# A fused attention and two feed-forward layers on one core: loads issued by two queues, mask patterns on two engines, and another block order at the start

## The chip, the cores and the metric

The kernel runs on one core of a Trainium2 chip, as one launch. The metric is device time in microseconds (us); the figure given for a kernel is the median of its runs. The engines are TensorE (PE in the profile; its weight loads are PEld), VectorE (DVE), ScalarE (ACT), GpSimd (POOL) and SyncE (SP), which here does little but issue DMA transfers.

## What is computed

All inputs are float32, but for two int64 words and the weights, which are float64.

```python
def _attn_ref(q, k, v, n_global, n_local):          # q, k, v: (2, 8, 768, 64)
    scores = scale * np.matmul(q, k.transpose(0, 1, 3, 2))
    rel = pos[:, None] - pos[None, :]
    is_global = pos[None, :] < int(n_global)         # 8
    is_local = (rel >= 0) & (rel < int(n_local))     # 96
    keep = is_global | is_local
    dist = np.where(is_global & ~is_local, float(n_local), np.abs(rel))
    slopes = 2.0 ** (-8.0 * (np.arange(H) + 1) / H)
    scores = np.where(keep, scores - slopes[:, None, None] * dist[None, :, :], -1000000000.0)
    ... softmax over the keys, times v ...
def _moe_ref(x, w_in, w_out):                        # (1536, 512) x (512, 2048), then x (2048, 512)
    h = x @ w_in
    return (h * (1.0 / (1.0 + np.exp(-h)))) @ w_out
def _moe2_ref(x, w_in, w_out):
    h = x @ w_in
    return (h * np.clip(h + 3.0, 0.0, 6.0) / 6.0) @ w_out
```

The result is `_moe2_ref(_moe_ref(attention))`.

## The kernel before

**Attention.** A query sees only the keys of the last 96 positions and the first 8, so the work goes in units: one batch entry, one half of the sequence (384 positions, three blocks of 128) and one pair of heads. There are 16 units, four pairs of heads for each half. A block of queries is scored against 256 columns (the 96 positions ahead of the block, 32 global keys, and its own 128 keys), or, for block 0 of a first half, against 128 (`width`). One loop counts slots `n`; slot `n` belongs to unit `n // 3`, step `n % 3`.

- `loads(u)` issues a unit's keys (`rk`, two transfers, one for each head), earlier keys (`kp`) and queries (`rq`, two transfers). Units 0, 1 and 2 are loaded ahead of the loop, unit u + 3 in unit u's step 1. `loads_v` does the values.
- `stage_a(u, 0)` transposes the keys on TensorE and copies them on ScalarE (L350, tile `kt`), `stage_a(u, 1)` the queries (L331, tile `qt`). Unit u + 1 is staged during unit u. `scores(u)`, at step 0, waits for `kt` and `qt`. It writes blocks 0 and 1 of a head into one PSUM bank (tag S) and block 2 into another (tag o). A matmul in float32 takes two passes, each an instruction of its own in the profile, so a unit's scores are 12 instructions.
- `exponentials(u, t)` adds the bias of block `t` on VectorE and takes the row minimum (L379, tile `z`, the negated scores), then ScalarE takes the exponential (L383). `normalise` divides on GpSimd (L393), blocks 0 and 1 at step 1, block 2 at step 2. `turn` transposes a unit's weights one unit later and `values` multiplies them by v.

**Mask patterns.** `positions` and `patterns` make two masks of distances from the words `n_global` and `n_local`, which the program reads at run time: `distA` (256 columns) and `distB` (128 columns, for block 0 of a first half). In `patterns` every step is VectorE's (L277 to L295). The temporaries lie in the two buffers of tile `z`, which units 0 and 1 take over. `biases(p)` multiplies both masks by the slopes of a head pair on GpSimd (L314, tiles `nbA` and `nbB`). `beyond` (L300 to L305) sets a flag for a general fallback; it is called in slot 30, and what reads the flag comes in slot 77.

**Weights.** The weights are float64 words and are decoded by hand in pieces of 128 x 512: ScalarE takes the absolute value (`upper`, L103) and the low word (`lower`, L107), VectorE shifts and masks (L992 to L1009), GpSimd multiplies and adds (L126, L134). Each step of a piece is put into a slot; `ahead` (L734) says how many slots before the piece's first use its decoding begins. For the first piece `ahead` is PRE = 17, so it begins in slot 0. Raw pieces have two buffers, and three pieces are requested ahead of the loop.

**Feed-forward.** From slot 17 on, pieces of the first layer's matmuls (`h_piece`, `y_piece`) are put between the attention steps; after the attention they fill the program to its end. Each product is done as three, with high and low parts of the operands.

**Order.** Within the attention loop the instructions of TensorE, ScalarE and GpSimd keep the order of the program; those of VectorE and SyncE are placed by a planner ahead of the launch. After it VectorE too keeps the program's order. Instructions of the loop can be placed between those that are written ahead of it. Each engine executes its list in order.

Of the kernel before, what the change touches and what calls it, by code (L numbers as in the profile page):

```python
# [12 lines left out]
I32 = mybir.dt.int32  # L13
# [15 lines left out]
def attention_ffn_kernel(ctx, tc, q, k, v, n_global, n_local, w_in1, w_out1, w_in2, w_out2, out):  # L29
# [17 lines left out]
    ident = keep.tile([P, P], F32, name="ident", tag="ident")  # L47
    nval = keep.tile([P, 2], F32, name="nval", tag="nval")
    flag = keep.tile([P, 1], I32, name="flag", tag="flag")
    three = keep.tile([P, 1], F32, name="three", tag="three")  # L50

    main = ExitStack()
# [102 lines left out]
    def fast(l, c):  # L155

        return c > (2, 1)[l]
# [61 lines left out]
    W = 2 * P  # L219
    SP = P + G  # L220

    def loads(u):
        b, half, p = units[u]
        s0 = half * TB
        rk = apool.tile([P, HB, 2, D], F32, name=f"rk{u}", tag="rk")
        kp = apool.tile([P, 2, D], F32, name=f"kp{u}", tag="kp")
        rq = apool.tile([P, HB, 2, D], F32, name=f"rq{u}", tag="rq")
        hs = slice(2 * p, 2 * p + 2)
        for h in range(2):
            nc.sync.dma_start(rk[:, :, h, :], k[b, 2 * p + h, s0:s0 + TB].rearrange("(t p) d -> p t d", p=P))  # L230
        if half:
            nc.sync.dma_start(kp[:G0], k[b, hs, s0 - G0:s0, :].rearrange("h p d -> p h d"))
            nc.sync.dma_start(kp[G0:], k[b, hs, :G, :].rearrange("h p d -> p h d"))
        else:
            nc.sync.dma_start(kp[:G], k[b, hs, :G, :].rearrange("h p d -> p h d"))
        for h in range(2):
            nc.sync.dma_start(rq[:, :, h, :], q[b, 2 * p + h, s0:s0 + TB].rearrange("(t p) d -> p t d", p=P))
        raw[u] = [rk, kp, rq, None, None]

    def loads_v(u):  # L240
# [15 lines left out]
    slopes = [2.0 ** (-8.0 * (h + 1) / H) for h in range(H)]  # L256
    FAR = 1e9 / slopes[-1]

    small = cpool.tile([P, 5], F32, name="small", tag="small")
    t1 = apool.tile([P, HB, 2, W], F32, name="pat1", tag="z", bufs=ZB)[:, 0]  # L260
    t2 = apool.tile([P, HB, 2, W], F32, name="pat2", tag="z", bufs=ZB)[:, 0]
    rel, tmp, glob, col = distA, t2[:, 0, :], t2[:, 1, :P], t2[:, 1, P:]

    def positions():

        reli, coli = t1[:, 0, :].bitcast(I32), t1[:, 1, :P].bitcast(I32)
        nc.gpsimd.iota(reli[:, :P], pattern=[[-1, P]], base=G0, channel_multiplier=1)
        nc.gpsimd.iota(reli[:, P:], pattern=[[-1, P]], base=0, channel_multiplier=1)
        nc.gpsimd.iota(coli, pattern=[[1, P]], base=0, channel_multiplier=0)
        nc.vector.tensor_copy(rel, reli)  # L270
        nc.vector.tensor_copy(col, coli)
        nc.vector.tensor_scalar(out=tmp, in0=rel, scalar1=0.0, scalar2=None, op0=ALU.is_ge)

    def patterns():

        low, up, high = nwords[:, :, 0], nwords[:, :, 1], small[:, 0:2]
        nc.vector.scalar_tensor_tensor(out=high, in0=low, scalar=0.0, in1=up, op0=ALU.is_lt, op1=ALU.add)  # L277
        nc.vector.scalar_tensor_tensor(out=nval, in0=high, scalar=4294967296.0, in1=low, op0=ALU.mult, op1=ALU.add)
        ng, nl = nval[:, 0:1], nval[:, 1:2]
        nc.vector.tensor_scalar(out=glob, in0=col, scalar1=ng, scalar2=None, op0=ALU.is_lt)  # L280
        nc.vector.scalar_tensor_tensor(out=tmp, in0=rel, scalar=nl, in1=tmp, op0=ALU.is_lt, op1=ALU.mult)

        def mask(dist, kept):
            nc.vector.tensor_scalar(out=kept, in0=kept, scalar1=-FAR, scalar2=FAR, op0=ALU.mult, op1=ALU.add)
            nc.vector.tensor_tensor(out=dist, in0=dist, in1=kept, op=ALU.max)


        nc.vector.scalar_tensor_tensor(out=distB, in0=rel[:, P:], scalar=nl, in1=tmp[:, P:], op0=ALU.subtract, op1=ALU.mult)
        nc.vector.tensor_scalar(out=distB, in0=distB, scalar1=nl, scalar2=None, op0=ALU.add)
        nc.vector.tensor_tensor(out=col, in0=tmp[:, P:], in1=glob, op=ALU.max)  # L290
        mask(distB, col)

        nc.vector.tensor_copy(tmp[:, G0:P], glob[:, :G])
        nc.vector.tensor_scalar(out=rel[:, G0:P], in0=rel[:, G0:P], scalar1=0.0, scalar2=nl, op0=ALU.mult, op1=ALU.add)
        mask(rel, tmp)  # L295

    def beyond():

        fl, ng, nl = small[:, 2:5], nval[:, 0:1], nval[:, 1:2]
        nc.vector.tensor_scalar(out=fl[:, 0:1], in0=nl, scalar1=1.0, scalar2=None, op0=ALU.is_lt)  # L300
        nc.vector.tensor_scalar(out=fl[:, 1:2], in0=nl, scalar1=float(NLOC_MAX), scalar2=None, op0=ALU.is_gt)
        nc.vector.tensor_scalar(out=fl[:, 2:3], in0=ng, scalar1=float(NGLOB_MAX), scalar2=None, op0=ALU.is_gt)
        nc.vector.tensor_tensor(out=fl[:, 0:1], in0=fl[:, 0:1], in1=fl[:, 1:2], op=ALU.add)
        nc.vector.tensor_tensor(out=fl[:, 0:1], in0=fl[:, 0:1], in1=fl[:, 2:3], op=ALU.add)
        nc.vector.tensor_copy(flag, fl[:, 0:1])  # L305
# [3 lines left out]
    def biases(p):  # L309

        nbs[p] = [cpool.tile([P, 2, w], F32, name=f"{n}{p}", tag=f"{n}{p}") for n, w in (("nbB", P), ("nbA", W))]
        for nb, dist in zip(nbs[p], (distB, distA)):
            for h in range(2):
                nc.gpsimd.tensor_scalar(out=nb[:, h, :], in0=dist, scalar1=slopes[2 * p + h], scalar2=1.0, op0=ALU.mult, op1=ALU.mult)  # L314


    KW = P + HB * SP
# [36 lines left out]

    zt, mnt, smt, ptt, scored = {}, {}, {}, {}, {}

    def width(u, t):
        return P if units[u][1] == 0 and t == 0 else W

    def scores(u):  # L360

        kt, qt = tr[u]
        two, one = ([bank(tag, f"psS{u}_{tag}{h}") for h in range(2)] for tag in "So")
        place = {(h, t): one[h][:, :W] if t == 2 else two[h][:, t * W:(t + 1) * W] for h in range(2) for t in range(HB)}
        for t in range(HB):
            for h in range(2):
                hs = slice(h * D, (h + 1) * D)
                o = P if width(u, t) == P else t * SP
                nc.tensor.matmul(place[h, t], qt[hs, t * P:(t + 1) * P], kt[hs, o:o + W], start=True, stop=True)
        scored[u] = place  # L370
        zt[u] = apool.tile([P, HB, 2, W], F32, name=f"z{u}", tag="z", bufs=ZB)
        mnt[u] = apool.tile([P, HB, 2], F32, name=f"mn{u}", tag="mn")
        smt[u] = apool.tile([P, HB, 2], F32, name=f"sm{u}", tag="sm")
# [21 lines left out]

    def turn(u):
        z = zt.pop(u)
        for t in range(HB):
            n = width(u, t) // P
            ps = bank("tr", f"psT{u}_{t}").rearrange("p (h c q) -> p h c q", h=2, c=2)  # L400
            for h in range(2):
                for c in range(n):
                    nc.tensor.transpose(ps[:, h, c, :], z[:, t, h, c * P:(c + 1) * P], ident)
            pt = apool.tile([P, 2, 2, P], F32, name=f"pt{u}_{t}", tag="pt", bufs=3)
            if t == 1:
                nc.scalar.copy(pt[:, :, :n, :], ps[:, :, :n, :])
            else:
                nc.vector.tensor_copy(pt[:, :, :n, :], ps[:, :, :n, :])
            ptt[u, t] = pt

    def values(u):
        b, half, p = units[u]
        rk, kp, rq, rv, vp = raw[u]
        ps = bank("tr", f"psO{u}")
        for t in range(HB):
            pt = ptt.pop((u, t))
            n = width(u, t) // P
            for c in range(n):
# [5 lines left out]
        nc.scalar.copy(hi, ps[:, :TB])  # L424
        return lambda: nc.vector.tensor_tensor(out=lo, in0=ps[:, :TB], in1=hi.bitcast(F32), op=ALU.subtract)  # L425

    def warm_up(n):

        for _ in range(n):
            nc.tensor.matmul(bank("f", "psW"), warm[:, :P], warm, start=True, stop=True)  # L430

    NS = HB * len(units)
    queue, late, rests, now = {}, {}, {}, [0]
# [4 lines left out]
    def attention_loop(n):  # L438
# [3 lines left out]
        if u < len(units):  # L442
            if t == 0:
                scores(u)
                if u + 1 < NP:
                    biases(u + 1)
            exponentials(u, t)
            if t:
                normalise(u, *((0, 2), (2, 3))[t - 1])
        if t == 0 and 0 <= u - 2 < len(units):  # L450
            at(n + 1, values(u - 2))
            if u < len(units):
                loads_v(u)
        if n == 30:
            beyond()
        for f in rests.pop(n, []):
            f()
        if n == 2:
# [272 lines left out]


    for n, (i, j) in enumerate(pieces):
        ahead = ((PRE, 11, 5, -1), (33, 27, 21, 15))[i][j] if i < 2 else (17, 13, 9, 5)[j] if chunks[i] == (1, 1) else ((20, 15, 11, 6), (18, 14, 9, 2))[fast(*chunks[i])][j]  # L734
        for off, f in decode(n):
            slots.setdefault(when(first_piece[chunks[i]]) - ahead + off, []).append(f)
        if j == 1 and fast(*chunks[i]):
# [3 lines left out]
    with tc.manual_schedule(engines=None):  # L741
        nc.vector.memset(three, 3.0)
        warm = fpool.tile([P, 512], F32, name="warm", tag="a")
        nc.vector.memset(warm, 0.0)
        warm_up(3)
        for i, ap in enumerate((n_global, n_local)):
            nc.sync.dma_start(nwords[:, i, :], ap.bitcast(I32).partition_broadcast(P))
        loads(0)
        make_identity(nc, ident)
        positions()  # L750
        loads(1)
# [29 lines left out]
    with tc.manual_schedule(engines={E.PE, E.Activation, E.Pool, E.DVE}):  # L781
# [5 lines left out]
        for n in range(end, when(len(stream) - 1) + 2):  # L787
            if n == when(first_piece[0, 3]):
                ready[0] = 2
            for l, c, early in ((0, 2, 0), (1, 1, 6)):  # L790
                if n == when(first_piece[l, c]) - early:
                    block_sums(l, n, n + early + 12)
            loop(n)
            if n == PRE + 60:
                general = nc.values_load(flag[0:1, 0:1], min_val=0, max_val=2)
    second_half.close()
# [245 lines left out]
```

## Time and profile before

| | |
|---|---|
| Time, median of 3 runs | 624.74 us |
| lowest and highest | 624.72 and 626.45 us |
| the profiled execution: time, span | 625.65 us, 623.5 us |
| TensorE busy in the span | 605.3 us (97%), 3128 matmul instructions |
| VectorE busy | 470.6 us (75%) |
| ScalarE busy | 414.7 us (67%) |
| GpSimd busy | 158.0 us (25%) |

The span runs from the first to the last instruction of the program; the profiled execution's time has about 2 us more around it. Busy shares are averages over the span. TensorE's ends are modelled, since its matmuls are pipelined. In a timeline the time in square brackets is how long the engine was idle ahead of an instruction, with what released it.

### The profile page before, as it was taken

How to read it: one execution, taken by the hardware profiler on the slowest of the kernel's cores; microseconds unless marked ns; L12 is line 12 of the kernel's file. 1: busy time of each engine (PE TensorE's matmuls, PEld its weight loads, DVE VectorE, ACT ScalarE, POOL GpSimd, SP SyncE). 2: the span in 40 equal slices, each digit the busy share in tenths (PEclk: the TensorE clock that was granted, in tenths of full speed). 3: DMA queues.
4: the chain of work that ended last, by engine and by line, in shares of the span. 5: the costliest groups of instructions: out<-in, count | busy, mean ns of one | idle time of the engine just before them, and what ended most of it. 6: DMA issues, size and time to landing. Idle time of an engine off the chain costs nothing.

```text
span 623.5 us, 9408 instructions
## 1 busy us (share of the span) xinstructions
PE 605.3 (97%) x3128; PEld 494.9 (79%) x3128; DVE 470.6 (75%) x1044; ACT 414.7 (67%) x863; POOL 158.0 (25%) x233
## 2 busy tenths in 40 slices
PE   8899999999999999999999989999999999999996
PEld 3577788898887888888888868887788888888885
DVE  6888888725697776767665789987979696969453
ACT  4888888655576666666656766756667676767660
POOL 3877566820111111111111210011111111111100
PEclk9999999999999999999999999999999999999999
DMA  7767655484776768777876772378577868786544
GB/s 176 178 157 167 155 143 124 138 181 114 159 150 153 182 149 183 155 180 155 183 156 147 173 171 70 126 198 189 124 177 157 184 153 181 155 185 138 102 110 165
DMA packets 81622, 97.29 MB, mean 156 GB/s; under 512 B 55456, under 2 KB 55456, under 8 KB 81312
## 3 DMA queue, kind: packets, MB, share of 16 engines
q0 software_dynamic: 12576, 45.09, 38.6%
q1 hardware_dynamic: 68992, 51.53, 28.3%
q8 instruction: 27, 0.44, 0.3%
q14 instruction: 27, 0.22, 0.1%
HBM read 46.27 MB, written 3.15 MB: 79 GB/s over the span
## 4 chain that ended last, share of the span: by engine, by line
PE 36%; issue 25%; POOL 5%; DVE 2%; DMA 2%; ACT 1%; POOLq 0%; ACTq 0%; SPq 0%; DVEq 0%
PE psY L662 20%; PE psH L489 9%; POOL y L691 5%; PE psP_b L570 3%; PE psP_c L570 2%; PE psP_a L570 2%; DMA y<-st 1%; DMA raw<-in_moe_w_in_dram 1%; ACT st L687 0%; DVE g L520 0%; DVE da L1004 0%; DVE wol L148 0%; DVE u L587 0%; DVE dc L134 0%; ACT da L103 0%
## 5 line engine op out<-in xcount | busy, mean ns | idle before, releaser
L691 POOL DMA_DIRECT2D y<-st x78 | 66.9, 857 | 364.6 <-ACT st L687 359.4
L687 ACT COPY st<-psY 128x512 f32<-128x512 f32 x156 | 91.3, 585 | 52.1 <-PE psY L662 48.0
L489 PE MATMUL psH<-xh,wih 128*128 128x512 f32 (+1 forms) x216 | 83.0, 384 | 2.2 <-DVE g L520 1.8
L489 PE MATMUL psH<-xl,wih 128*128 128x512 f32 (+1 forms) x216 | 82.6, 383 | 0.1
L489 PE MATMUL psH<-xh,wil 128*128 128x512 f32 (+1 forms) x216 | 82.5, 382 | 0.0
L662 PE MATMUL psY<-gh,woh 128*128 128x512 f32 (+1 forms) x160 | 61.4, 384 | 0.6 <-DVE mn L379 0.6
L662 PE MATMUL psY<-gh,wol 128*128 128x512 f32 (+1 forms) x160 | 60.6, 379 | 0.0
L662 PE MATMUL psY<-gl,woh 128*128 128x512 f32 (+1 forms) x160 | 60.5, 378 | 0.0
L662 PE MATMUL psY<-woh,gh 128*128 128x512 f32 x144 | 56.1, 390 | 0.4 <-ACT gh L526 0.4
L662 PE MATMUL psY<-woh,gl 128*128 128x512 f32 x144 | 56.1, 390 | 0.2 <-DVE gl L533 0.2
L662 PE MATMUL psY<-wol,gh 128*128 128x512 f32 x144 | 56.0, 389 | 0.0
L383 ACT ACTIVATE z<-z,mn 128x256 f32<-128x256 f32 (+1 forms) x96 | 46.4, 488 | 10.9 <-DVE mn L379 10.6
L393 POOL TENSOR_SCALAR z<-z,sm 128x256 f32<-128x256 f32 (+1 forms) x96 | 43.5, 471 | 32.3 <-DVE sm L389 25.0
L489 PEld LDWEIGHTS psH<-xh,wih 128*128 128x128 f32 x216 | 40.6, 188 | 10.4 <-DVE g L520 2.2
L103 ACT ACTIVATE da<-raw 128x512 f32<-128x512 f32 x64 | 43.0, 672 | 6.8 <-DMA raw<-in_moe_w_in_dram 5.6
L489 PEld LDWEIGHTS psH<-xl,wih 128*128 128x128 f32 x216 | 40.5, 188 | 7.9 <-DVE xl L425 0.5
L1004 DVE SCALAR_TENSOR_TENSOR da<-raw,da 128x512 int32<-128x512 int32 x64 | 46.0, 718 | 1.0
L489 PEld LDWEIGHTS psH<-xh,wil 128*128 128x128 f32 x216 | 40.6, 188 | 7.5 <-POOL wil L148 0.3
L992 DVE TENSOR_SCALAR da<-da 128x512 f32<-128x512 f32 x64 | 29.1, 454 | 16.2 <-ACT da L103 16.1
L587 DVE TENSOR_TENSOR u<-psP_c,u 128x512 f32<-128x512 f32 x22 | 15.1, 687 | 34.5 <-ACT u L581 34.5
L511 ACT ACTIVATE a<-psH 128x512 f32<-128x512 f32 (+1 forms) x24 | 14.2, 590 | 40.5 <-PE psH L489 38.7
L530 DVE SCALAR_TENSOR_TENSOR gl<-a,gh 128x512 fp32r<-128x512 f32 (+1 forms) x34 | 23.2, 681 | 22.3 <-ACT gh L524 22.0
(187 smaller groups left out, 1499.8 us busy)
## 6 DMA issues: line engine op xcount, KB each, us to landing
y<-st POOLq DMA_DIRECT2D x78, 512.0 KB, 4.9
raw<-in_moe_w_in_dram SPq DMA_DIRECT2D x32, 512.0 KB, 4.3
raw<-in_moe_w_out_dram SPq DMA_DIRECT2D x32, 512.0 KB, 3.6
rk<-in_k_dram SPq DMA_DIRECT2D x32, 96.0 KB, 3.2
rq<-in_q_dram SPq DMA_DIRECT2D x32, 96.0 KB, 2.7
rv<-in_v_dram SPq DMA_DIRECT2D x32, 96.0 KB, 2.6
out_dram<-y SPq DMA_DIRECT2D x12, 256.0 KB, 2.3
xf<-xh SPq DMA_DIRECT2D x2, 1024.0 KB, 4.8
```

Source lines behind the costliest of these rows:

```text
L103: nc.scalar.activation(out=t["a"], in_=raws[n][:, :, 1].bitcast(F32), func=AF.Abs)
L383: nc.scalar.activation(out=z[:, t, h, :w], in_=z[:, t, h, :w], func=AF.Exp, bias=mn[:, t, h:h + 1], scale=-1.0, accum_out=sm[:, t, h:h + 1])
L393: nc.gpsimd.tensor_scalar(out=z[:, t, h, :w], in0=z[:, t, h, :w], scalar1=smt[u][:, t, h:h + 1], scalar2=1.0, op0=ALU.mult, op1=ALU.mult)
L489: nc.tensor.matmul(ps, a[:, kt, js], x[:, kt, n0:n1], start=n == 0, stop=n == 3 * KT - 1)
L530: nc.vector.scalar_tensor_tensor(out=gl[:, j, :], in0=t["a"], scalar=2.0, in1=gh[:, j, :].bitcast(F32), op0=ALU.mult, op1=ALU.subtract)
L570: nc.tensor.matmul(ps, a[:, 2 * k + q, f * P:(f + 1) * P], x, start=p in (1, 5) and n == 0, stop=n == 5, skip_group_check=True)
L587: nc.vector.tensor_tensor(out=u, in0=st["c"], in1=u, op=ALU.add)
L662: nc.tensor.matmul(ps[:, :rhs.shape[1]], lhs, rhs, start=n == 0, stop=n == 3 * FC - 1)
L687: nc.scalar.copy(st[:, m % 2, :], part)
L691: late.setdefault(n, []).append(lambda: nc.gpsimd.dma_start(y, st, accum_op=ALU.add))
L992: nc.vector.tensor_scalar(out=a, in0=a, scalar1=as_float(897 << 20), scalar2=as_float((1151 << 20) - 1), op0=ALU.max, op1=ALU.min)
L1004: nc.vector.scalar_tensor_tensor(out=ai, in0=w1, scalar=-0x40000000, in1=ai, op0=ALU.bitwise_and, op1=ALU.bitwise_or)
```

## The change

The two words and unit 0's queries are issued on ScalarE's queue instead of SyncE's. The third pair of warm-up passes has 128 columns instead of 512. `patterns` is rewritten: VectorE makes `distA`, GpSimd (`g`) makes `distB`, with a temporary `near`; both masks add a large distance where a key is not seen, in place of a maximum. The temporaries fill both z buffers for longer, since `rel` now lies in the first one. The two wide biases of the first head pair are made by VectorE. The blocks of a first-half unit are scored, reduced, normalised and transposed in the order 1, 2, 0. The first weight piece is decoded three slots later. `beyond` moves from slot 30 to slot 73.

```diff
-    def loads(u):
+    def loads(u, other=None):
...
         for h in range(2):
-            nc.sync.dma_start(rq[:, :, h, :], q[b, 2 * p + h, s0:s0 + TB].rearrange("(t p) d -> p t d", p=P))
+            (other or nc.sync).dma_start(rq[:, :, h, :], q[b, 2 * p + h, s0:s0 + TB].rearrange("(t p) d -> p t d", p=P))
...
-    t1 = apool.tile([P, HB, 2, W], F32, name="pat1", tag="z", bufs=ZB)[:, 0]
+    pat = apool.tile([P, HB, 2, W], F32, name="pat1", tag="z", bufs=ZB)
+    t1 = pat[:, 0]
     t2 = apool.tile([P, HB, 2, W], F32, name="pat2", tag="z", bufs=ZB)[:, 0]
-    rel, tmp, glob, col = distA, t2[:, 0, :], t2[:, 1, :P], t2[:, 1, P:]
+    tmp, glob, col = t2[:, 0, :], t2[:, 1, :P], t2[:, 1, P:]
+    rel, near = pat[:, 1, 0, :], pat[:, 1, 1, :P]
...
-        nc.vector.tensor_scalar(out=glob, in0=col, scalar1=ng, scalar2=None, op0=ALU.is_lt)
-        nc.vector.scalar_tensor_tensor(out=tmp, in0=rel, scalar=nl, in1=tmp, op0=ALU.is_lt, op1=ALU.mult)
-
-        def mask(dist, kept):
-            nc.vector.tensor_scalar(out=kept, in0=kept, scalar1=-FAR, scalar2=FAR, op0=ALU.mult, op1=ALU.add)
-            nc.vector.tensor_tensor(out=dist, in0=dist, in1=kept, op=ALU.max)
-
-
-        nc.vector.scalar_tensor_tensor(out=distB, in0=rel[:, P:], scalar=nl, in1=tmp[:, P:], op0=ALU.subtract, op1=ALU.mult)
-        nc.vector.tensor_scalar(out=distB, in0=distB, scalar1=nl, scalar2=None, op0=ALU.add)
-        nc.vector.tensor_tensor(out=col, in0=tmp[:, P:], in1=glob, op=ALU.max)
-        mask(distB, col)
-
+        g, own = nc.gpsimd, slice(P, W)
+        g.tensor_scalar(out=near, in0=rel[:, own], scalar1=nl, scalar2=1.0, op0=ALU.subtract, op1=ALU.mult)
+        nc.vector.scalar_tensor_tensor(out=tmp, in0=rel, scalar=nl, in1=tmp, op0=ALU.is_ge, op1=ALU.max)
+        nc.vector.tensor_scalar(out=glob, in0=col, scalar1=ng, scalar2=None, op0=ALU.is_ge)
         nc.vector.tensor_copy(tmp[:, G0:P], glob[:, :G])
         nc.vector.tensor_scalar(out=rel[:, G0:P], in0=rel[:, G0:P], scalar1=0.0, scalar2=nl, op0=ALU.mult, op1=ALU.add)
-        mask(rel, tmp)
+        nc.vector.scalar_tensor_tensor(out=distA, in0=tmp, scalar=FAR, in1=rel, op0=ALU.mult, op1=ALU.add)
+
+
+        g.tensor_tensor(out=near, in0=near, in1=tmp[:, own], op=ALU.mult)
+        g.tensor_tensor(out=near, in0=rel[:, own], in1=near, op=ALU.subtract)
+        g.tensor_tensor(out=glob, in0=glob, in1=tmp[:, own], op=ALU.mult)
+        g.tensor_scalar(out=glob, in0=glob, scalar1=FAR, scalar2=1.0, op0=ALU.mult, op1=ALU.mult)
+        g.tensor_tensor(out=distB, in0=glob, in1=near, op=ALU.add)
...
             for h in range(2):
-                nc.gpsimd.tensor_scalar(out=nb[:, h, :], in0=dist, scalar1=slopes[2 * p + h], scalar2=1.0, op0=ALU.mult, op1=ALU.mult)
+                engine = nc.vector if p == 0 and dist is distA else nc.gpsimd
+                engine.tensor_scalar(out=nb[:, h, :], in0=dist, scalar1=slopes[2 * p + h], scalar2=1.0, op0=ALU.mult, op1=ALU.mult)
...
+    def order(u):
+        return (0, 1, 2) if units[u][1] else (1, 2, 0)
...
-        for t in range(HB):
+        for t in order(u):
             for h in range(2):
                 hs = slice(h * D, (h + 1) * D)
...
-            exponentials(u, t)
+            exponentials(u, order(u)[t])
             if t:
-                normalise(u, *((0, 2), (2, 3))[t - 1])
+                t0 = order(u)[2 * t - 2]
+                normalise(u, t0, t0 + 3 - t)
...
-        if n == 30:
-            beyond()
...
-        ahead = ((PRE, 11, 5, -1), (33, 27, 21, 15))[i][j] if i < 2 else (17, 13, 9, 5)[j] if chunks[i] == (1, 1) else ((20, 15, 11, 6), (18, 14, 9, 2))[fast(*chunks[i])][j]
+        ahead = ((PRE - 3, 11, 5, -1), (33, 27, 21, 15))[i][j] if i < 2 else (17, 13, 9, 5)[j] if chunks[i] == (1, 1) else ((20, 15, 11, 6), (18, 14, 9, 2))[fast(*chunks[i])][j]
...
-        warm_up(3)
+        warm_up(2)
+        warm_up(1, P)
         for i, ap in enumerate((n_global, n_local)):
-            nc.sync.dma_start(nwords[:, i, :], ap.bitcast(I32).partition_broadcast(P))
-        loads(0)
+            nc.scalar.dma_start(nwords[:, i, :], ap.bitcast(I32).partition_broadcast(P))
+        loads(0, nc.scalar)
...
+            if n == PRE + 56:
+                beyond()
```

`turn` and `values` take the blocks in `order(u)` too.

## Rows read from the trace of the kernel before

**Rows 1.** Windows: span, busy us (instructions) per engine, clock, DMA share, GB/s.

```profile
0.00:5.70 5.70, 4.14 (x4) 1.00 (x4) 2.17 (x11) 1.28 (x1) 1.26 (x9) 1.00 0.37 77
5.00:10.00 5.00, 4.36 (x22) 2.41 (x21) 3.38 (x18) 0.97 (x2) 2.50 (x7) 1.00 0.84 217
10.00:15.00 5.00, 4.67 (x27) 2.40 (x23) 4.21 (x20) 4.58 (x15) 0.69 (x2) 1.00 1.01 251
40.00:120.00 80.00, 76.62 (x682) 64.12 (x677) 67.44 (x252) 67.01 (x209) 56.32 (x90) 1.00 0.60 144
120.00:600.00 480.00, 476.69 (x2140) 394.91 (x2141) 361.11 (x641) 314.25 (x559) 77.11 (x88) 1.00 0.70 158
```

**Rows 2.** Timeline of SyncE's queue: start us, us, issue.

```profile
0.76 0.39 SPq L747 DMA_DIRECT2D nwords<-in_n_global_dram  x1
...
1.67 0.96 SPq L230 DMA_DIRECT2D rk<-in_k_dram  x2
...
3.20 0.97 SPq L237 DMA_DIRECT2D rq<-in_q_dram  x2
4.21 1.02 SPq L230 DMA_DIRECT2D rk<-in_k_dram  x2
```

**Rows 3.** Tile views, issue to landing: the two words, then unit 0's queries.

```profile
DMA to landing us min/median/max: 2.6/2.9/3.3
...
DMA to landing us min/median/max: 2.7/2.7/2.8
```

**Rows 4.** Source view of the warm-up passes: durations ns, first four, then last.

```profile
L430 PE MATMUL psW<-warm x4: 1061/1141/1222, 1.5 to 4.7; 128*128 128x512 f32 x4
...
L430 PE MATMUL psW<-warm x1: 593/593/593, 6.6 to 6.6; 128*128 128x512 f32 x1
```

**Rows 5.** Timeline of TensorE, unit 0.

```profile
7.02 0.49 PE L329 MATMUL psA<-ident,rk 128*128 128x128 f32 x3
...
8.74 1.13 PE L369 MATMUL psS_S<-kt,qt 64*128 64x256 f32 x8 [0.58 <-ACT qt L331]
```

**Rows 6.** Timeline of VectorE: words, last step of the wide mask, first score.

```profile
4.64 0.16 DVE L277 SCALAR_TENSOR_TENSOR small<-nwords 128x2 f32<-128x2 int32 x1 [2.27 <-DMA nwords<-in_n_local_dram]
...
7.79 0.42 DVE L285 TENSOR_TENSOR distA<-distA,pat 128x256 f32<-128x256 f32 x1
...
10.02 0.29 DVE L379 CUSTOM_DVE_ANT_0 z<-psS_S,nbB 128x128 f32<-128x128 f32 x1 [1.57 <-POOL nbA L314]
```

**Rows 7.** Timeline of GpSimd's biases; groups of GpSimd to 60 us (busy, mean).

```profile
7.31 1.43 POOL L314 TENSOR_SCALAR nbB<-distB 128x128 f32<-128x128 f32 x4 [5.42 <-DVE pat L293]
8.81 1.62 POOL L314 TENSOR_SCALAR nbA<-distA 128x256 f32<-128x256 f32 x4
...
L134 POOL TENSOR_TENSOR dc<-dc,da 128x512 f32<-128x512 f32 x3 | 3.8, 1273 | 0.2
```

**Rows 8.** Timeline of ScalarE, 0 to 14 us.

```profile
0.76 1.28 ACT L350 ACT_TABLE_LOAD   x1 [0.76 <-PEq L1024]
7.72 0.48 ACT L350 COPY kt<-psA 128x384 f32<-128x384 f32 x1 [5.68 <-PE psA L338]
...
11.67 0.67 ACT L103 ACTIVATE da<-raw 128x512 f32<-128x512 f32 x1
...
13.23 0.46 ACT L331 ACTIVATE qt<-psA 128x384 f32<-128x384 f32 x1
```

**Rows 9.** Timeline of TensorE and VectorE, unit 1.

```profile
13.75 1.13 PE L369 MATMUL psS_S<-kt,qt 64*128 64x256 f32 x8 [0.27 <-ACT qt L331]
...
14.91 0.29 DVE L379 CUSTOM_DVE_ANT_0 z<-psS_S,nbB 128x128 f32<-128x128 f32 x1 [0.38 <-PE psS_S L369]
```

**Rows 10.** Timeline of SyncE's queue and TensorE, unit 3's keys.

```profile
17.07 0.36 SPq L90 DMA_DIRECT2D raw<-in_moe_w_out_dram  x1
17.53 0.92 SPq L230 DMA_DIRECT2D rk<-in_k_dram  x2
...
21.64 0.52 PE L329 MATMUL psA<-ident,rk 128*128 128x128 f32 x3 [0.46 <-DMA rk<-in_k_dram]
```

More of the change, by code (lines that the diff above doesn't have):

```diff
@@ L49, in attention_ffn_kernel @@
     flag = keep.tile([P, 1], I32, name="flag", tag="flag")
+    beyonds = keep.tile([P, 3], F32, name="beyonds", tag="beyonds")
     three = keep.tile([P, 1], F32, name="three", tag="three")
@@ L257, in attention_ffn_kernel @@
     FAR = 1e9 / slopes[-1]
-    small = cpool.tile([P, 5], F32, name="small", tag="small")
-    t1 = apool.tile([P, HB, 2, W], F32, name="pat1", tag="z", bufs=ZB)[:, 0]
+    small = cpool.tile([P, 2], F32, name="small", tag="small")
+    pat = apool.tile([P, HB, 2, W], F32, name="pat1", tag="z", bufs=ZB)
+    t1 = pat[:, 0]
     t2 = apool.tile([P, HB, 2, W], F32, name="pat2", tag="z", bufs=ZB)[:, 0]
-    rel, tmp, glob, col = distA, t2[:, 0, :], t2[:, 1, :P], t2[:, 1, P:]
+    tmp, glob, col = t2[:, 0, :], t2[:, 1, :P], t2[:, 1, P:]
+    rel, near = pat[:, 1, 0, :], pat[:, 1, 1, :P]
     def positions():
@@ L271, in positions @@
         nc.vector.tensor_copy(col, coli)
-        nc.vector.tensor_scalar(out=tmp, in0=rel, scalar1=0.0, scalar2=None, op0=ALU.is_ge)
+        nc.vector.tensor_scalar(out=tmp, in0=rel, scalar1=0.0, scalar2=None, op0=ALU.is_lt)
     def patterns():
@@ L279, in patterns @@
         ng, nl = nval[:, 0:1], nval[:, 1:2]
-        nc.vector.tensor_scalar(out=glob, in0=col, scalar1=ng, scalar2=None, op0=ALU.is_lt)
-        nc.vector.scalar_tensor_tensor(out=tmp, in0=rel, scalar=nl, in1=tmp, op0=ALU.is_lt, op1=ALU.mult)
-        def mask(dist, kept):
-            nc.vector.tensor_scalar(out=kept, in0=kept, scalar1=-FAR, scalar2=FAR, op0=ALU.mult, op1=ALU.add)
-            nc.vector.tensor_tensor(out=dist, in0=dist, in1=kept, op=ALU.max)
-        nc.vector.scalar_tensor_tensor(out=distB, in0=rel[:, P:], scalar=nl, in1=tmp[:, P:], op0=ALU.subtract, op1=ALU.mult)
-        nc.vector.tensor_scalar(out=distB, in0=distB, scalar1=nl, scalar2=None, op0=ALU.add)
-        nc.vector.tensor_tensor(out=col, in0=tmp[:, P:], in1=glob, op=ALU.max)
-        mask(distB, col)
+        g, own = nc.gpsimd, slice(P, W)
+        g.tensor_scalar(out=near, in0=rel[:, own], scalar1=nl, scalar2=1.0, op0=ALU.subtract, op1=ALU.mult)
+        nc.vector.scalar_tensor_tensor(out=tmp, in0=rel, scalar=nl, in1=tmp, op0=ALU.is_ge, op1=ALU.max)
+        nc.vector.tensor_scalar(out=glob, in0=col, scalar1=ng, scalar2=None, op0=ALU.is_ge)
         nc.vector.tensor_copy(tmp[:, G0:P], glob[:, :G])
         nc.vector.tensor_scalar(out=rel[:, G0:P], in0=rel[:, G0:P], scalar1=0.0, scalar2=nl, op0=ALU.mult, op1=ALU.add)
-        mask(rel, tmp)
+        nc.vector.scalar_tensor_tensor(out=distA, in0=tmp, scalar=FAR, in1=rel, op0=ALU.mult, op1=ALU.add)
[4 more added lines that the diff above has]
+        g.tensor_tensor(out=distB, in0=glob, in1=near, op=ALU.add)
     def beyond():
-        fl, ng, nl = small[:, 2:5], nval[:, 0:1], nval[:, 1:2]
+        fl, ng, nl = beyonds, nval[:, 0:1], nval[:, 1:2]
         nc.vector.tensor_scalar(out=fl[:, 0:1], in0=nl, scalar1=1.0, scalar2=None, op0=ALU.is_lt)
@@ L397, in turn @@
         z = zt.pop(u)
-        for t in range(HB):
+        for t in order(u):
             n = width(u, t) // P
@@ L404, in turn @@
             pt = apool.tile([P, 2, 2, P], F32, name=f"pt{u}_{t}", tag="pt", bufs=3)
-            if t == 1:
+            if t == order(u)[1]:
                 nc.scalar.copy(pt[:, :, :n, :], ps[:, :, :n, :])
@@ L414, in values @@
         ps = bank("tr", f"psO{u}")
-        for t in range(HB):
+        for t in order(u):
             pt = ptt.pop((u, t))
@@ L425, in values, with warm_up @@
         return lambda: nc.vector.tensor_tensor(out=lo, in0=ps[:, :TB], in1=hi.bitcast(F32), op=ALU.subtract)
-    def warm_up(n):
+    def warm_up(n, m=512):
         for _ in range(n):
-            nc.tensor.matmul(bank("f", "psW"), warm[:, :P], warm, start=True, stop=True)
+            nc.tensor.matmul(bank("f", "psW")[:, :m], warm[:, :P], warm[:, :m], start=True, stop=True)
     NS = HB * len(units)
```

## The prediction

> **What bounds the kernel now.** I read the windows first. From 40 to 120 us TensorE is busy 76.62 of 80 us, and from 120 to 600 us 476.69 of 480 [rows 1]. Nothing in this change takes work off it there, so the change can only move the point at which the full stretch begins. All of its edits but one small one act before 25 us, so I went through that part by the timeline, engine by engine, and asked at each step which wait ends last.
>
> The start has three strands. Strand one is TensorE: three warm-up pairs, then the transposes of unit 0's keys at 7.02 and the first scores at 8.74, which waited for ScalarE's copy of the queries [rows 5]. The copy of the keys waited for TensorE until 7.72 [rows 8]. Strand two is the loads: SyncE issues words, keys, queries and then unit 1 without a pause, one every half microsecond [rows 2]; the queries were issued at 3.20 and landed 2.7 to 2.8 us after each issue, about 6.4 for the second [rows 3]. Strand three is the patterns: VectorE starts on the words at 4.64 and ends the wide mask at 8.21, and GpSimd turns it into biases at 8.81 and after [rows 6, 7]. The first score read on VectorE comes at 10.02, put down to a GpSimd bias [rows 6]. That row is easily over-read. Unit 1 shows the same step without a bias to wait for: scores from 13.75, read at 14.91, released by the scores [rows 9], 1.16 us later. Unit 0's scores would by this have been read at 8.74 + 1.16 = 9.90. The patterns cost 0.12 us, no more; both strands end together, and both must be shortened.
>
> **The change, part by part.** *Loads.* SyncE loses four issues. Its keys move from 1.67 to 0.76, 0.91 earlier; unit 1 moves from 4.21 to 0.76 + (3.20 − 1.67) = 2.29 or so, 1.9 earlier, and everything queued behind it on SyncE (first weight pieces, values, unit 2) likewise [rows 2]. On ScalarE the words keep their issue times, and the queries follow at about 1.7 and 2.1. Ahead of them stands at most the table load, 1.28 us [rows 8]: it carries the line of the first copy, L350, so I place it behind the issues, ending near 4, when ScalarE has nothing else until 7. If it went first, words and queries would be 1.28 us later; the queries would then land about 6.2, still in time. The queries stand in line behind the words, whose second transfer took 3.3 us [rows 3], to 4.5; they need about 0.4 us each, as their two landings do, so 5.3 at best and, with unit 1's keys sharing the engines, 6.4 at worst, where they are now.
>
> The row on the transfer engines bears on this: their share is 0.84 from 5 to 10 us and 1.01 from 10 to 15 [rows 1], so unit 2's loads, issued in that stretch, are held by the engines and not by the issue. I therefore count 0.9 us for them, the earlier start of the first transfer, not 1.9. The Trainium skill ("DMA: Bandwidth & Descriptors", section "Issuing engines are not separate DMA queues") says that transfers from several engines run on the same 16 engines and interleave, and that a second issuer saves only issue time; by that rule the lead of 1.9 us is worth nothing wherever the engines are full, and the share of 1.01 agrees.
>
> *Warm-up.* The third pair runs from 5.77 and holds TensorE until 7.02. A quarter as many columns makes 1.25 us into 0.3 to 0.45, so the keys' transposes start near 6.2: 0.8 earlier. Keys are there by then (issued 0.9 earlier, and they were not waited for before), queries are needed from 6.8. The rest of the strand is unchanged, 1.72 us from transposes to scores [rows 5]: first scores at 7.95, the bounds being 7.85 and, with no gain, 8.75.
>
> *Patterns.* Words to wide mask took 3.57 us on VectorE, with beyond's six operations in the gaps. About half of the steps remain ahead of the wide mask, so it is done near 6.5; the two biases that VectorE now makes itself cost what the like-shaped last mask step does, 0.42 each [rows 6]: 7.3 to 7.5. On GpSimd five operations form a chain after the mask at about 5.8. A two-input operation of four times their width takes 1.27 us, and four narrow biases took 1.43 us [rows 7], so one costs 0.32 to 0.5: narrow mask at 7.4 to 8.3, its biases 0.7 later, with the order 1, 2, 0 needed only about 11. There is a new wait: the pattern buffers are the two buffers of z, and now both are in use until GpSimd's last step, so the first score read waits for that too. It has over 1 us of cover; that is gone if the words come 1 us later.
>
> *Order 1, 2, 0.* Blocks 0 and 1 of a head share one bank. In unit 1 the read waited until all eight passes of the shared banks were done (13.75 + 1.13 = 14.88, read at 14.91) although the first four serve the block that was read [rows 9]. Now block 0 is scored last, so the first read waits for all twelve passes, 0.4 to 0.55 us more in each of the eight first-half units. First read: 7.95 + 1.16 + 0.4 = 9.5 instead of 10.02. Half of the gain at the start is spent here.
>
> *First weight piece three slots later.* Its Abs of 0.67 us at 11.67 sits in ScalarE's order ahead of unit 1's query copy at 13.23 [rows 8]. Moved, it takes 0.55 off (its 0.67 less an overlap of about 0.1), and the first read gives 0.4 more (0.5, less 0.1 for its wider block): unit 1's scores at 12.8 instead of 13.75. But it returns in unit 1, which is no shorter of work there: Abs +0.6 on the chain to unit 2's scores, the bank wait +0.4, against about 0.2 for the two equally wide reads that no longer make ScalarE wait. Unit 2's scores thus keep 0.95 − 0.6 − 0.4 + 0.2, about 0.1 us, of the lead. The four VectorE and three GpSimd steps of this piece move with it, into gaps.
>
> *Unit 3.* TensorE waited 0.46 us for its keys at 21.64; they had been issued at 17.53, right behind the third weight piece at 17.07 [rows 10]. With loads 0.9 or more ahead this goes: −0.46. What follows it in the unit (query wait, transposes, VectorE's copies) I put at −0.3, between 0 and −0.6, since waits of this size stand after it.
>
> *Beyond* moves to a slot where TensorE sets the pace and VectorE has spare time; its reader comes four slots later. Nothing.
>
> Sum: −0.1 − 0.46 − 0.3 = −0.85 us at the start of the full stretch, and from there on no wait is tied to an absolute time, so it is kept. Against the profiled execution (623.5 us of span, 625.65 in all) that is 624.8; that execution lies 0.9 above the median of the runs, 624.74, from which I forecast **623.9**.
>
> **Rivals.** *All of the lead survives* (0.24). If unit 2 and 3 were really held by issue, 1.9 us plus the 0.46 come through: 622.4. For it: SyncE issues without a pause for tens of microseconds. Against: the share of 1.01, and ScalarE's chain, which doesn't get shorter.
>
> *It is all given back* (0.12): bank wait and moved Abs eat the rest, and unit 3's keys are not earlier; 624.7.
>
> *The third weight piece blocks SyncE* (0.09). Its buffer is freed by the first piece's decode, now three slots later, about 19 by the steps above (unit 2's scores, then the piece's second pass on ScalarE). SyncE works in order: it is at that piece at 17.07 − 1.9 = 15.2, and if it stands there to 19, unit 3's keys are issued near 19.4, 1.9 later than before, and TensorE gets them 1.9 after 21.6; less the 0.1 and what slack is left, +0.9: 625.6. It decides as soon as the piece still precedes unit 3's keys in SyncE's order; the planner could put the keys first.
>
> *The slow TensorE* (0.07), on the other side. The granted clock reads 1.00 in all stretches [rows 1], but the first four warm-up passes took 1.06 to 1.22 us and the last 0.59 [rows 4]: the lower of the levels 1.2 and 2.4 GHz and the higher one, with an engine that was idle at first and then busy with these passes. With the third pair cut, it is busy only to about 6.2 ahead of short transposes. If the rise doesn't come, each transpose and score pass costs about 0.1 more (three transposes take 0.49, eight passes 1.13 [rows 5], a part of it latency): seven transposes, twelve passes, unit 1's seven transposes and a little after them, 0.7 + 1.2 + 0.7 + 0.2, less the gain of 0.85: about +1.95, 626.7. It decides if the first scores start after 8.6. The Trainium skill ("TensorE: Matmul & The Clock Gate", Part 1) has the throttled state as the default and activity as what lifts it, which is this rival's rule; the passes agree, the clock column doesn't show it.
>
> **How the numbers follow.** The forecast's own case holds 0.48, with 623.0 to 624.6 as its range. 0.3%, which is 1.9 us, is about what a measurement of this kernel tells from no change. Faster by more (under 622.9): nearly all of the first rival and the edge of the forecast, 0.26. Slower by more (over 626.6): the slow TensorE, and the blocked queue if it costs twice my price, 0.09. Within: 0.65. For 8 in 10 I take 621.9 to 626.2, from a little past the best case to halfway into the slow one.
>
> **What would show it.** Right: keys transposed near 6.2; scores at about 7.9; first score read at 9.4 to 9.6, released by the scores, not by a bias; unit 1's scores near 12.8 and unit 2's near 18.3; no wait for keys near 21. Wrong: passes of 0.2 us where 0.1 stood; words landing after 5.5; unit 2's scores a full microsecond early (then the first rival); SyncE idle ahead of the third weight piece; or a TensorE that waits differently between 40 and 120 us, where I expect none of it.

## The result, and the profile after

| | before | after |
|---|---|---|
| median, same chip | 625.05 us (624.72 to 626.45, 4 runs) | 634.12 us (633.71 to 634.37, 4 runs) |
| profiled execution: time, span | 625.65, 623.5 us | 634.37, 632.3 us |

The changed kernel is slower: ratio 1.0136, 95% interval 1.0122 to 1.0149. The forecast was 623.9. The span grew by 8.8 us, and three places hold it. Unit 15's scores, the last ones, start at 113.96 us (109.61 before): 4.35 lost in the attention. The last matmul starts at 625.35 (617.79): 7.56, so 3.2 more in the feed-forward stretch. The rest, 1.25, lies behind the last matmul.

The start first, by engine. TensorE's timeline, units 0 and 1 (answers to [rows 5, 9]):

```profile
6.34 0.85 PE L331 MATMUL psA<-ident,rk 128*128 128x128 f32 x3
...
8.71 0.70 PE L374 MATMUL psS_S<-kt,qt 64*128 64x256 f32 x4 [0.58 <-ACT qt L333]
9.24 0.60 PE L374 MATMUL psS_o<-kt,qt 64*128 64x256 f32 x4
9.67 0.60 PE L374 MATMUL psS_S<-kt,qt 64*128 64x256 f32 x4
...
14.07 0.70 PE L374 MATMUL psS_S<-kt,qt 64*128 64x256 f32 x4 [0.63 <-DVE sm L394]
```

The keys' transposes start 0.7 earlier, but three of them take 0.85 instead of 0.49 us. That is nearly the pace of the lower of the clock's two levels, although the granted clock reads 1.00 from 5 to 10 us; the engine had done only warm-up passes before. The scores, at the usual rate, start where they did.

GpSimd's timeline, the new chain and its biases (answers to [rows 7]):

```profile
5.34 1.02 POOL L284 TENSOR_SCALAR pat<-pat,nval 128x128 f32<-128x128 f32 x1 [3.47 <-DVE nval L281]
6.45 0.46 POOL L292 TENSOR_TENSOR pat<-pat,pat 128x128 f32<-128x128 f32 x1
...
8.44 0.45 POOL L296 TENSOR_TENSOR distB<-pat,pat 128x128 f32<-128x128 f32 x1
8.98 1.19 POOL L316 TENSOR_SCALAR nbB<-distB 128x128 f32<-128x128 f32 x4
```

VectorE's timeline, unit 0's reads of the scores (answers to [rows 6]):

```profile
9.97 0.42 DVE L384 CUSTOM_DVE_ANT_0 z<-psS_o,nbA 128x256 f32<-128x256 f32 x1 [1.73 <-POOL nbB L316]
...
10.32 0.42 DVE L384 CUSTOM_DVE_ANT_0 z<-psS_o,nbA 128x256 f32<-128x256 f32 x1
...
10.67 0.42 DVE L384 CUSTOM_DVE_ANT_0 z<-psS_S,nbA 128x256 f32<-128x256 f32 x1
...
11.01 0.28 DVE L384 CUSTOM_DVE_ANT_0 z<-psS_S,nbB 128x128 f32<-128x128 f32 x1
```

ScalarE's timeline, the table load and the first exponentials of units 0 and 1 (answers to [rows 8]):

```profile
2.70 1.28 ACT L352 ACT_TABLE_LOAD   x1 [2.70 <-issue]
...
11.20 0.51 ACT L388 ACTIVATE z<-z,mn 128x256 f32<-128x256 f32 x1 [2.54 <-POOL nbA L316]
...
16.51 0.51 ACT L388 ACTIVATE z<-z,mn 128x256 f32<-128x256 f32 x1 [1.72 <-DVE mn L384]
```

These two are the main reading. ScalarE keeps the program's order, 1, 2, 0, and its first exponential is of block 1. VectorE's order is the planner's, and it reads block 2 (`psS_o`) first, both heads, then blocks 1 and 0 in turn. So block 1's first minimum is there at 11.1 and ScalarE begins at 11.20 instead of 10.36; its row names a bias, but what is late is VectorE's order. ScalarE's first exponential in the kernel before, which is of block 0:

```profile
10.36 0.40 ACT L383 ACTIVATE z<-z,mn 128x128 f32<-128x128 f32 x1 [1.67 <-DVE mn L379]
```

ScalarE's waits for the minima up to 120 us after the change (us in total, times, longest):

```profile
ACT z L388 <- DVE mn L384: 16.3, 12, 2.2
```

The same of the kernel before:

```profile
ACT z L383 <- DVE mn L379: 10.6, 11, 1.7
```

The windows, with the columns of [rows 1]:

```profile
40.00:120.00 80.00, 74.56 (x662) 61.96 (x661) 66.87 (x251) 65.36 (x206) 54.64 (x87) 1.00 0.55 134
120.00:600.00 480.00, 477.96 (x2147) 392.53 (x2146) 361.94 (x651) 312.44 (x558) 79.61 (x93) 1.00 0.68 157
```

Behind 120 us TensorE is busy even longer than before, 477.96 of 480 after 476.69 [rows 1], and yet falls behind: a slower pace also fills part of its waits. Busy time can't show it; counting instructions in stretches without a gap does. Windows of TensorE alone, after:

```profile
240.00:335.00 95.00, 95.00 (x416) 1.00 0.73 166
480.00:600.00 120.00, 120.00 (x524) 1.00 0.69 153
```

The same windows of the kernel before:

```profile
240.00:335.00 95.00, 95.00 (x421) 1.00 0.74 166
480.00:600.00 120.00, 120.00 (x531) 1.00 0.71 155
```

Fewer matmuls at the same granted clock: by the start times in the first window 229.6 ns from one to the next after, 226.7 before. TensorE's timeline shows which are slow; after:

```profile
262.07 0.39 PE L574 MATMUL psP_a<-xh,wil 128*128 128x512 f32 x1
262.30 0.63 PE L666 MATMUL psY<-g,woh 128*128 128x512 f32 x2
262.77 0.40 PE L666 MATMUL psY<-g,wol 128*128 128x512 f32 x1
263.00 0.63 PE L666 MATMUL psY<-g,woh 128*128 128x512 f32 x2
```

The same products in the timeline of the kernel before:

```profile
257.19 0.39 PE L570 MATMUL psP_a<-xh,wil 128*128 128x512 f32 x1
257.42 0.62 PE L662 MATMUL psY<-g,woh 128*128 128x512 f32 x2
257.88 0.39 PE L662 MATMUL psY<-g,wol 128*128 128x512 f32 x1
258.10 0.62 PE L662 MATMUL psY<-g,woh 128*128 128x512 f32 x2
```

Three matmuls take 0.70 us from 262.30 to 263.00, about 233 ns each, and 0.68 before, 227 each; `psP_a` just ahead keeps 0.23. The slow runs come at the same products in chunk after chunk of the weights. A run begins at, or one matmul ahead of, a product of one operand from the late tiles (`g` of the second token block, `ws`, `t2` to `t4`, which lie at the right side of the SBUF) and one from the left side (`xh`, the weights), and takes neighbours with it.

### The profile page after: what moved, and what is told of

Same layout as the page of the kernel before. It is cut to its first block, busy times and chain, and to the rows that moved or that the text cites. A ratio compares the mean times of both kernels' runs of the same rounds, so it can differ in the third digit from the quotient of the medians.

```text
span 632.3 us, 9416 instructions
## 1 busy us (share of the span) xinstructions
PE 608.9 (96%) x3128; PEld 495.1 (78%) x3128; DVE 471.5 (75%) x1040; ACT 414.8 (66%) x863; POOL 160.7 (25%) x237
## 4 chain that ended last, share of the span: by engine, by line
PE 36%; issue 25%; POOL 5%; DVE 2%; DMA 2%; ACT 1%; POOLq 0%; ACTq 0%; SPq 0%; DVEq 0%
PE psY L666 20%; PE psH L493 9%; POOL y L695 5%; PE psP_b L574 3%; PE psP_c L574 2%; PE psP_a L574 2%; DMA y<-st 1%; DMA raw<-in_moe_w_in_dram 1%; ACT st L691 0%; DVE g L524 0%; DVE da L1011 0%; DVE wol L149 0%; DVE u L591 0%; DVE dc L135 0%; ACT da L104 0%
## 5 line engine op out<-in xcount | busy, mean ns | idle before, releaser
L999 DVE TENSOR_SCALAR da<-da 128x512 f32<-128x512 f32 x64 | 30.4, 476 | 17.1 <-ACT da L104 17.0
```

The source lines that it names most:

```text
L999: nc.vector.tensor_scalar(out=a, in0=a, scalar1=as_float(897 << 20), scalar2=as_float((1151 << 20) - 1), op0=ALU.max, op1=ALU.min)
```

## The experiments

**The left side 32 bytes higher, in the kernel before.** The change also gives `beyond` a tile of its own, `beyonds`, for three columns that lay in `small` before; the diff ahead doesn't show these lines. The tile stands in the constants pool, which rounds each tile up to 32 bytes and on which the left side is stacked.

```diff
+beyonds = keep.tile([P, 3], F32, name="beyonds", tag="beyonds")
-fl, ng, nl = small[:, 2:5], nval[:, 0:1], nval[:, 1:2]
+fl, ng, nl = beyonds, nval[:, 0:1], nval[:, 1:2]
```

> The kernel before with one edit: the three flag columns of the range test get a tile of their own of 12 bytes per partition in the constants pool, as in the changed kernel; every instruction and its order stay. All tiles of the left side of the SBUF (activations, weights, gate results) then lie 32 bytes higher, those of the right side (the sums and products' operands of the late stage) stay. Theory 1 (placement): products that take one operand from the left side and one from the late tiles run at 231 to 236 ns instead of 226.7; of the 8.8 us lost in the span some 3.2 to 4.4 lie behind 120 us, so 627.9 to 629.1 us and an unchanged attention stretch (first psH at 41.4). Theory 2 (the slower matmuls come from what runs beside them, the order of VectorE and the transfers): no change, 624.7 to 625.3.

631.32 us (629.85 to 632.01), ratio 1.0089 [1.0073, 1.0104]. The windows:

```profile
240.00:335.00 95.00, 95.00 (x416) 1.00 0.73 166
480.00:600.00 120.00, 120.00 (x524) 1.00 0.70 154
```

The same counts as after the whole change: the place alone makes the matmuls slow. The time is above the theory's 629.1. In the profiled execution (630.16) 1.2 us is something else, a lower clock at unit 3, in a window of TensorE; why the median lies another 1.2 higher stays open:

```profile
26.00:30.00 4.00, 4.00 (x33) 0.65 0.72 187
```

**64 bytes, in the changed kernel.**

```diff
-beyonds = keep.tile([P, 3], F32, name="beyonds", tag="beyonds")
+beyonds = keep.tile([P, 16], F32, name="beyonds", tag="beyonds")
```

> The changed kernel with its new tile at 64 bytes per partition instead of 12, of which three columns are used: the left side now lies 64 bytes above its place in the kernel before, not 32. Theory 1 (placement, by the place modulo 64): matmul pitch back to 226.7 ns behind 120 us, 629.7 to 630.9 us; by any shift at all: 634 as the changed kernel. Theory 2 (what runs beside): 633.7 to 634.4.

633.70 us (633.29 to 634.65), 416 and 527 matmuls: still slow, in part of the places. (Its first scores were slow as well, unit 1's 1.4 later than in the changed kernel.) The place modulo 64 bytes isn't it; that guess fell.

**The old block order in the changed kernel.**

```diff
-return (0, 1, 2) if units[u][1] else (1, 2, 0)
+return (0, 1, 2)
```

> The changed kernel with the query blocks of the first half in the order 0, 1, 2 again; loads on ScalarE's queue, split patterns, the late range test and the new tile stay. Theory 1 (block order costs the 4.35 us of the attention stretch, because VectorE reads the last bank first and ScalarE waits): 629.5 to 630.5 us, unit 12's scores at 88.2 give or take 0.4. Rival (the stretch lost its time to the slow pattern chain on GpSimd and the clock of the first transposes): 633 or more, unit 12's scores still near 92.

629.86 us (629.25 to 630.61), unit 12's scores at 87.85 (92.56 with the new order), 416 and 523 matmuls. 634.12 − 629.86 = 4.26 us are the order's.

**The new block order alone, in the kernel before.** `order(u)` is put into the loops of `scores`, `turn`, `values` and the calls of `exponentials` and `normalise`, as in the diff of the change.

> The kernel before with the block order 1, 2, 0 in first-half units alone (scores, exponentials, normalising, turns, values). Theory 1: about 4 us slower, 628.4 to 629.4 us, growth in units 0 to 3 and 8 to 11 only, matmul pitch behind 120 us unchanged at 226.7 ns. Rival (the order costs nothing by itself): 624.7 to 625.3.

630.87 us (630.62 to 633.31), ratio 1.0088 [1.0071, 1.0106], 421 and 531 matmuls. It costs 5.4, over the 4 expected. In the profiled execution unit 0's first scores are late (9.48), and part of the cost is again a lower clock, at unit 3, in a window of TensorE:

```profile
26.00:30.00 4.00, 2.28 (x13) 0.79 0.40 89
```

**The changed kernel with its tiles in the old place.**

```diff
-nval = keep.tile([P, 2], F32, name="nval", tag="nval")
-beyonds = keep.tile([P, 3], F32, name="beyonds", tag="beyonds")
+nvals = keep.tile([P, 5], F32, name="nval", tag="nval")
+nval, beyonds = nvals[:, 0:2], nvals[:, 2:5]
```

> The changed kernel with its three range-test columns in the same tile as the two read words (20 bytes where 8 stood; the pool rounds both up to 32), so that every tile lies where it lay in the kernel before. Placement theory: pitch behind 120 us back to 226.7 ns and 421 and 531 matmuls in 240 to 335 and 480 to 600 us; what is left is the order of the blocks, so about the 630.9 us of the order put alone into the kernel before; by subtraction of what the shift alone cost (5.9), 628.2. So 628.2 to 630.9. If the slow matmuls of the changed kernel had a second cause, it stays above 632.

630.80 us (629.47 to 633.33), 420 and 531 matmuls: 3.3 us less than the changed kernel, by place alone. (The two were not run side by side; the price is taken up below.)

**Old place and old order.** Both edits together. (The first weight piece is decoded three slots later here, as in the change, not earlier as the expectation has it.)

> The same, and the first-half blocks in the order 0, 1, 2 again: what is left of the change is the loads on ScalarE's queue, the split patterns, the shorter warm-up, the earlier first weight piece and the later range test. If placement and block order are all that the change cost, its 0.36 us lead at unit 12 in the run with the old order (87.85 after 88.21) survives and it takes 624.5 to 625.4 us, against 625.4 before. Rival (the lead is given back later, or the parts cost something): 625.5 to 626.5.

626.45 us (624.77 to 627.22), ratio 0.9998 [0.9984, 1.0013]. Place and order were the whole loss, and the rest of the change is worth nothing that can be measured. That its lead would show was a miss; in the profiled execution the clock took it, and unit 1's scores came at 14.72 instead of the 13.10 of the changed kernel with the old order:

```profile
9.00:11.00 2.00, 2.00 (x12) 0.50 0.95 197
```

**Order 1, 2, 0, with a bank of its own for block 1.**

```diff
-place = {(h, t): one[h][:, :W] if t == 2 else two[h][:, t * W:(t + 1) * W] ...
+alone = 2 if units[u][1] else 1
+place = {(h, t): one[h][:, :W] if t == alone else two[h][:, (t > 0) * W:(t > 0) * W + W] ...
```

> The changed kernel in its old place in the SBUF and with the order 1, 2, 0 kept, but block 1 gets the PSUM bank of its own in first-half units and block 0 shares with block 2. Theory 1a (the order costs because the block that is wanted first shares a bank with the block scored last, so VectorE's planner puts another block ahead and ScalarE waits for it): VectorE reads block 1 first, unit 12's scores at 88 to 89, 624.5 to 626 us. Rival 1b (the order itself costs, by the half-width block at the end of the unit or the normalising of two wide blocks together): unit 12's scores near 92.5 and 628.2 to 630.9 us, as with the shared bank.

627.12 us (625.29 to 629.92), unit 12's scores at 88.57 against 92.30 with the shared bank. VectorE's timeline, its first score read:

```profile
9.32 0.42 DVE L385 CUSTOM_DVE_ANT_0 z<-psS_o,nbA 128x256 f32<-128x256 f32 x1 [0.98 <-PE psS_o L375]
```

ScalarE's timeline, its first exponential:

```profile
9.79 0.51 ACT L389 ACTIVATE z<-z,mn 128x256 f32<-128x256 f32 x1 [1.37 <-DVE mn L385]
```

`psS_o` is now block 1; it is read first, while the other passes still run, and ScalarE begins at 9.79 instead of 11.06 (old place, shared bank; 11.20 in the changed kernel). The waits for minima fall from 18.7 us (old place, shared bank) to 9.3. The shared bank is most of what the order cost: 630.80 − 627.12 = 3.7 us of 630.80 − 626.45 = 4.35. The rest is within the spread of these runs. The time lies 1.1 above the end of the expected range; its profiled execution, 625.62, lies in it.

**Both sides moved, in the kernel before.** The late tiles go 224 bytes down.

```diff
 (with the 12-byte tile, as in the first experiment)
 t1 = late_pool.tile([P, 2, FB], F32, name=f"t1f{l}", tag="u")
+late_pool.tile([P, 56], F32, name=f"room{l}", tag="room")
```

> The kernel before with its left side 32 bytes higher (as in the first experiment) and the tiles of the late stage 224 bytes lower: the distance between the two is then the old one modulo 256 bytes, while both lie at other places modulo 64. Relative theory (an operand of one side with one of the other is slow when their distance is not a multiple of 128 or 256 bytes): pitch back to 226.7 ns, 624.8 to 626 us. Absolute theory (the left side's own place counts): pitch 229.6 and 630.5 to 632 us, as with the left side shifted alone.

625.15 us (624.07 to 627.75), ratio 0.9989 [0.9972, 1.0006]. The windows:

```profile
240.00:335.00 95.00, 95.00 (x421) 1.00 0.72 166
480.00:600.00 120.00, 120.00 (x531) 1.00 0.69 155
```

All the speed is back, with both sides at new places: of the two theories only the one of their distance is left.

**128 and 256 bytes, in the kernel before.** The first experiment's tile as `[P, 32]` and as `[P, 64]`.

> The kernel before with its left side 128 bytes higher, all instructions unchanged, the late tiles at their place. If a distance between the two sides that is a multiple of 128 bytes is enough: pitch 226.7 ns and 624.8 to 626.5 us. If it must be a multiple of 256: pitch between 228 and 230 ns and 628 to 631.5 us.

> The kernel before with its left side 256 bytes higher. Relative theory, either modulus: pitch 226.7 ns, 624.8 to 626.5 us. If any shift that leaves the late tiles where they are costs (the old place being a lucky one by the absolute addresses): 628 to 631.5 us.

128: 628.89 us (628.35 to 630.65), ratio 1.0059 [1.0038, 1.0079], 416 and 525 matmuls. 256: 625.84 us (625.04 to 627.07), ratio 1.0005 [0.9994, 1.0016], 420 and 531.

**Two parts of the change alone, in the kernel before.** The words and first queries on ScalarE's queue; the split patterns (`positions`, `patterns` and `biases` of the change, the range test where it was).

> The kernel before with the words and the first queries issued by ScalarE's queue, nothing else. The forecast's step: first scores up to 0.8 earlier (7.95 after 8.74), unit 3's keys earlier. If the warm-up's length and not the queue sets the first scores, they stay within 0.3 us of 8.74; if the lead survives, unit 12's scores come 0.3 to 0.8 us before 88.21 and the time is 624.6 to 625.2; if the attention stretch has waits that absorb it, 625.2 to 626. If the longer closing steps of SyncE (1.2 us more between the last product and the end of the span) come from the moved loads, they show here; else they belong to the other parts.

> The kernel before with the mask patterns split over VectorE and GpSimd and the first wide bias table on VectorE, nothing else. In the changed kernel the chain on GpSimd ended at 8.9 and its first bias tables at 10.2. If GpSimd's chain is what held the first score read at 9.97, unit 0's first read comes here at 9.8 to 10.4 too, and unit 1's scores within 0.4 us of 13.75; 625 to 626.5 us. If the split frees VectorE as forecast (first read 9.5), unit 1's scores at 13.2 or earlier and 624.3 to 625.

Queue: 625.70 us, ratio 1.0002 [0.9990, 1.0014]; first scores at 8.81, unit 12's at 87.85. Patterns: 626.31 us, ratio 1.0011 [1.0002, 1.0021]; first score read at 10.23, unit 1's scores at 13.96. Neither shows a lead at the first units, and the patterns alone are, just clear of no change, 0.1% slower. The shorter warm-up and the later first weight piece were not run alone. That unit 12 is 0.3 to 0.4 early in both doesn't reach the time. Behind the last matmul's start the span has 6.0 and 7.2 us (5.7 before, 7.0 after, but 6.7 with 128 bytes alone): these closing steps vary from kernel to kernel, and what sets them stays open.

## Why the prediction was wrong

**"From there on no wait is tied to an absolute time, so it is kept", and "Beyond ... Nothing."** This failed first. The instructions of `beyond` cost nothing; the 12 bytes that it got did. In the compiled kernels' memory map, `xh` starts at byte 17120 of a partition and the first late tile at 172000, a distance of 605 times 256; all activations, weights and gate results of the left side lie a multiple of 256 bytes from all late tiles. The distance modulo 256, against matmuls from 480 to 600 us:

| distance modulo 256 | 0 | 224 | 192 | 128 | 0 | 0 |
|---|---|---|---|---|---|---|
| kernel | before | 32 up | 64 up (the changed kernel) | 128 up | 256 up | 32 up, late 224 down |
| matmuls | 531 | 524 | 527 | 525 | 531 | 531 |

Price: 634.12 − 630.80 = 3.3 us, and 629.86 − 626.45 = 3.4 with the old order. These compare runs of different times and chips; by the ratios to the kernel before beside each it is 0.52% and 0.69%, 3.3 and 4.3 us. The traces agree: from unit 15's scores to the last matmul's start it is 510.5 to 511.4 us in the five profiled kernels with another distance, and 506.9 to 508.2 in the nine with a multiple of 256. That it is the distance is shown; what collides inside is not. The prediction sought costs among instructions and waits; a new tile was neither. The Trainium skill ("SBUF — State Buffer", section "SBUF: two separate sides") says that TensorE's reads wait for nobody, and that weight loads have a read port of their own. The traces show a loss even so: with the same instructions, 1.3% fewer matmuls (524 of 531) fit where the tiles lay otherwise. Whether TensorE's own two reads meet there, or another engine's, no run shows.

**"Order 1, 2, 0 ... 0.4 to 0.55 us more in each."** The mechanism was named, but mis-sized, and left out of the sum: the bank wait is counted in the first two units and put at nothing, without a reason, in the other six, though eight times its own price is 3.2 to 4.4 us. The prediction let VectorE read block 1 late. The planner instead read block 2 while it waited, and ScalarE, whose order is the program's, stood still until VectorE came to block 1: its first exponential of unit 0 comes 1.27 us after the own-bank kernel's in the old place (11.06 and 9.79). Over the eight first-half units it is 92.30 − 88.57 = 3.7 at unit 12, and 3.7 in the time (630.80 − 627.12). Of this 26.99 − 24.23 = 2.8 is there at unit 3's scores and 33.23 − 29.99 = 3.2 at unit 4's, 0.8 for each of the first four units. Unit 2's scores were forecast at 18.3 and came at 20.03. The Trainium skill ("PSUM — Partial Sum Buffer", section "PSUM bank collisions raise a hardware error") wants readers guarded by bank, not by address; the order of the reads with the shared and with the own bank agrees.

**First scores at 7.95.** They came at 8.71. This is the condition of the rival of the slow TensorE (after 8.6), but only the transposes were slow; the scores ran at the higher level, so it took the gain of 0.8 and not the rival's 1.95. In single executions of other kernels the scores were slow too, and cost 1.4 and 1.6 us by unit 1 (with 64 bytes, and with old place and order, above).

**First score read at 9.5.** It came at 9.97. The row names a GpSimd bias, but the read is 0.13 after the last pass of block 2 (9.24 + 0.60 = 9.84), as it is 0.14 after its bank's last pass with the own bank (8.48 + 0.70 = 9.18, read at 9.32):

```profile
8.48 0.70 PE L375 MATMUL psS_o<-kt,qt 64*128 64x256 f32 x4 [0.59 <-ACT qt L333]
```

So the late scores set it. GpSimd's chain was late too: its first step took 1.02 us, over the bound of 0.5, with the words 0.24 later (4.88 after 4.64), and the chain ended at 8.89, not 7.4 to 8.3. But the cover that was counted for it held.

**Loads.** The steps held: keys at 0.74, unit 1 at 2.29, the table load behind the issues. The third weight piece went behind unit 3's keys (21.34 after 18.24), so SyncE didn't stand. But the lead alone was worth nothing (ratio 1.0002). That agrees with the rule of the Trainium skill ("DMA: Bandwidth & Descriptors", section "Issuing engines are not separate DMA queues") which the prediction weighed.

**The rival "all is given back"** is what the rest of the change did, in its number and not by its steps: in the changed kernel with the old order unit 5 is still 1.2 early (36.41 after 37.61), and unit 6 only 0.38 (44.88 after 45.26). Of TensorE's waits in between two are new, one of them for the first decoded weights, which are now decoded later; the rows of that kernel's waits (us in total, times, longest):

```profile
PE psH L493 <- POOL wil L149: 0.3, 1, 0.3
PE psO L426 <- DVE pt L413: 0.3, 1, 0.3
```

## What to carry to other kernels

Compare where the tiles lie, not only the instructions: a small tile ahead of a stack of big ones moves them all, and where TensorE is the bound, count matmuls per stretch, since busy time hides a slower pitch. When the order of consumers changes, look at which results share a PSUM bank, and let what is wanted first have a bank to itself; an engine that a planner orders may otherwise serve another block while an engine in program order waits. A price that is found for one unit belongs in the sum for every unit that pays it. A lead at the start is only worth what the waits behind it let through.

## What was not expected of the hardware

Here matmuls of 512 columns follow each other at 226.7 ns, and at about 233 ns in runs that mix operands of two regions whose distance isn't a multiple of 256 bytes (32, 64 and 128 bytes off were slow, 256 was not), at a granted clock of 1.00. Neighbours with both operands in one region are slow within such a run. And kernels with the same instructions can find another clock in their first 30 us: with the old order, unit 0's eight passes of the shared banks took 1.13 us in the changed kernel, and 2.00 in the old place, where the window from 9 to 11 us shows 0.50 and 1.6 us were lost by unit 1.
